# Cosine attention and a low-rank mixer: three query multiplies of the first batch on GpSimd, and the query and key copies of the same head pairs on VectorE alone

## The chip, the cores and the metric

The kernel runs on one core of one Trainium2 chip. The metric is the device time of one execution in microseconds (us). A time with "median" is the median of an experiment's timed runs; a profile shows one execution, and its span is some 2 us shorter than the time of the same run. The engines are called PE (TensorE), ACT (ScalarE), DVE (VectorE), POOL (GpSimd) and SP (SyncE); SBUF is the on-chip memory, PSUM the banks into which PE writes.

## The reference

```python
def _attn_ref(q, k, v, tau):                       # q, k, v: 8 x 12 x 448 x 64
    q_n = q / (np.linalg.norm(q, axis=-1, keepdims=True) + 1e-06)
    k_n = k / (np.linalg.norm(k, axis=-1, keepdims=True) + 1e-06)
    scores = np.matmul(q_n, k_n.transpose(0, 1, 3, 2)) / tau
    scores = scores - np.max(scores, axis=-1, keepdims=True)
    attn = np.exp(scores)
    attn = attn / (np.sum(attn, axis=-1, keepdims=True) + 1e-09)
    return np.matmul(attn, v)

def _moe_ref(x, U, V, w_ch1, w_ch2):               # x: 8 x 448 x 768, rank 32
    xt = x.transpose(0, 2, 1)
    h = xt @ U @ V
    u = x + h.transpose(0, 2, 1)
    ch = np.maximum(u @ w_ch1, 0.0) @ w_ch2        # 768 -> 3072 -> 768
    return u + ch
```

Twelve heads make six pairs (0 to 5) per batch. The change touches only batch 0, in the first 32 us of some 605.

## The kernel before

The kernel does not emit its instructions in the order of its source. It collects them as operations with an estimated duration and with dependences, and a small list scheduler simulates the five engines with these estimates when the kernel is built. The order it finds is then fixed for each engine. An operation marked "ACT/DVE" goes to whichever of the two the simulation finds free. So a change of one duration or one engine can rearrange everything behind it.

```python
def flip(stream, ins, n, into, part, deps, acq, rel, wide=1, eng="ACT/DVE", took=0.05):
    # PE transposes the blocks into PSUM, one copy brings them into qkT
    ...
    c = plan.add(Op(eng, any_t(n * len(ins) // wide, 2), None, deps=[o], acq=acq, rel=[tp],
                    prio=0.2, fast=True))
    c.fn = lambda: copy_op(c, *part(into(), tp.tile))
    return c
...
def scales(b, h0, h1, ld, ops, lo, ii, inv, pr, on, hold=()):
    # squares (ACT or DVE), sums (DVE), Ln and Exp (ACT), + EPS and reciprocal (DVE): inv, f32 in SBUF
    ...
def norm(b, p, ld, la, inv, a, deps, pr):          # one pair of heads
    ...
    def part(i, h0=0, h1=2):                       # i = 0: queries, i = 1: keys
        def fn():
            src = ...                              # 112 x 512, bf16, in SBUF
            sc = inv.tile[:, i, a + h0:a + h1, :].unsqueeze(3).to_broadcast([SCH, n, SC, D])
            ...
            nc.vector.tensor_mul(dst, src, sc)     # the unit queries or keys
        return plan.add(Op("DVE", dve_t(256 * (h1 - h0)), fn, deps=need + [deps[i]], acq=[xn],
                           rel=[ld, inv], prio=pr))
    ...
            done.append(flip(pe_tp, ..., [o], [qkT], [xn], 1, "ACT/DVE", 0.09 if first else 0.05))
```

The inverse norms are made for a third (four heads) at a time. Pairs 2 and 3 share a third, and so do pairs 4 and 5. Each pair then gives eight score matmuls and eight exponentials on ACT. GpSimd works through one list in the order of the source: it asks for all loads, and between them it clears tiles and casts the mixer's weights.

```python
    load_w1(0, 6)                                  # two of the four quarters of w1
    load_w1(6, 12)
    v_set = [plan.add(Op("POOL", 1.5, lambda t_=t_: set_v(t_)), pool_q) for t_ in v_t]
    consts = [ ...cast_u(0), cast_v, cast_u(1)... ]       # U and V to bf16
    state[0] = att(0)
    ...
    go(1, 0, 4)                                    # queries and keys of batch 1, heads 0 to 3
    load_w1(12, 18)                                # the third quarter
```

Of the kernel before, what the change touches and what calls it, by code (L numbers as in the profile page):

```python
# [204 lines left out]
def kernel(  # L205
# [12 lines left out]
    nc = tc.nc  # L218
# [95 lines left out]
    plan = Plan()  # L314
# [6 lines left out]
    pool_q = plan.stream("POOL")  # L321
# [7 lines left out]
    def dve_t(n, fast=1, fixed=0.065):  # L329
        return fixed + n * 0.00105 / fast  # L330
# [4 lines left out]
    def load(fn, busy, deps=(), acq=(), rel=(), late=2.0):  # L335
        return plan.add(Op("POOL", 0.71, fn, deps=deps, acq=acq, rel=rel,
                           lat=("in", busy, late)), pool_q)
# [7 lines left out]
    def load_w1(f0, f1):  # L345

        o = load(lambda: nc.gpsimd.dma_start(
            out=w1_sb[:, :, f0 * 128:f1 * 128],
            in_=moe_w_ch1.rearrange("(a p) f -> p a f", p=128)[:, :, f0 * 128:f1 * 128]),
            C * (f1 - f0) * 128 * 4 / 400e3)  # L350
        for f in range(f0, f1):
            w1_of[f] = o
# [8 lines left out]
    def flip(stream, ins, n, into, part, deps, acq, rel, wide=1, eng="ACT/DVE", took=0.05):  # L361


        tp = Slot(r_mm, 1)
        tp.own = True
        for z, x in enumerate(ins):
            def fn(z=z, x=x):
                if z == 0:
                    tp.tile = psum.tile([128, len(ins) // wide, n], BF, name="tp", tag="mm", bufs=3)
                m = 128 // wide  # L370
                nc.tensor.transpose(out=tp.tile[m * (z % wide):m * (z % wide + 1), z // wide, :], in_=x(),  # L371
                                    identity=ident[:n, :n])
            o = plan.add(Op("PE", took, fn, deps=deps + [id_set] if z == 0 else (), acq=[tp] + acq,
                            rel=rel if z == len(ins) - 1 else []), stream)
# [4 lines that stand above are left out]
# [5 lines left out]
    def load_qk(b, h0, h1, ld=None, lo=0, uses=None):  # L384

        ld = ld or Slot(r_ld, 4 if uses is None else uses)
        ops = [load(lambda i=i, src=src: nc.gpsimd.dma_start(  # L387
            out=ld.tile[:, i, lo:lo + h1 - h0, :],
            in_=src[b, h0:h1].rearrange("h (s c) d -> s h (c d)", c=SC)),
            (h1 - h0) * (0.31 if b else 0.35) + (1.2 if b == 0 and h0 == 4 and i == 0 else 0.0), acq=[ld], late=2.0 if b == 0 else LATE) for i, src in enumerate((q, k))]  # L390
        return ld, ops, lo
# [77 lines left out]
    def stats(b, h0, h1, ld, ops, lo, hold=()):  # L469

        pr = 0.3 + 0.03 * h0 if b == 0 else 4
        inv = Slot(r_inv, h1 - h0)
        o, _ = scales(b, h0, h1, ld, ops, lo, (0, 1), inv, pr, "DVE" if b else "ACT/DVE", hold)
        for p in range(h0 // 2, h1 // 2):
            o_ = norm(b, p, ld, lo + 2 * p - h0, inv, 2 * p - h0, {0: o, 1: o}, pr)
        return o_

    def stats_first(ld, ops):

        inv = Slot(r_inv, 3)  # L480
        done, ups = {}, []
        for i in range(2):
            done[i], up = scales(0, 0, 2, ld, ops, 0, (i,), inv, -1 - 0.1 * i, ("DVE", "ACT")[i])
            ups.append(up)
        return ups + norm(0, 0, ld, 0, inv, 0, done, -1)

    count = [0]

    def norm(b, p, ld, la, inv, a, deps, pr):


        by_pe = b < PE_BATCHES
        first = b == 0 and p == 0
        xn, qkT = Slot(r_xn, 3 if first else 2 if by_pe else 1), Slot(r_qkT, 8 if b == 0 else 7)
        need = [xn_set[count[0] % len(xn_t)]]
        count[0] += 1

        def part(i, h0=0, h1=2):
            def fn():
                n = h1 - h0  # L500
                src = ld.tile[:, i, la + h0:la + h1, :].rearrange("p h (c d) -> p h c d", d=D)
                sc = inv.tile[:, i, a + h0:a + h1, :].unsqueeze(3).to_broadcast([SCH, n, SC, D])
                if i == 0:
                    dst = xn.tile[:, 8:12, :].rearrange("p c (h d) -> p h c d", h=2)
                else:
                    dst = xn.tile.rearrange("p b e -> p (b e)")[:, 0:9 * 128].rearrange(
                        "p (h x) -> p h x", h=2)[:, h0:h1, 0:SC * 128].rearrange(
                        "p h (c e) -> p h c e", c=SC)[:, :, :, 0:D]
                nc.vector.tensor_mul(dst, src, sc)  # L509
            return plan.add(Op("DVE", dve_t(256 * (h1 - h0)), fn, deps=need + [deps[i]], acq=[xn],  # L510
                               rel=[ld, inv], prio=pr))

        if first:
            ops = [part(0), part(1, 0, 1), part(1, 1, 2)]
            blocks = [(8, 12, ops[0]), (0, 4, ops[1]), (4, 8, ops[2])]
        else:
            ops = [part(1), part(0)]
            blocks = [(0, 8, ops[0]), (8, 12, ops[1])]
        if not by_pe:
            done = [plan.add(Op("SP", 0.1, lambda: nc.sync.dma_start_transpose(  # L520
                out=qkT.tile, in_=xn.tile.rearrange("p b e -> p (b e)")), deps=ops, acq=[qkT],
                rel=[xn], prio=0, lat=("x", 0.05 * 84, LATE)))]
        else:
            done = []
            for b0, b1, o in blocks:
                done.append(flip(
                    pe_tp, [(lambda z=z: xn.tile[:, z, :]) for z in range(b0, b1)], SCH,
                    lambda: qkT.tile, (lambda t_, x, b0=b0, b1=b1: (t_[:, b0:b1, :], x)),
                    [o], [qkT], [xn], 1, "ACT/DVE", 0.09 if first else 0.05))
        got[b, p, "qkT"] = (qkT, lambda m: (done[0], done[1 + m // 4]) if first else done, done)  # L530
        return ops

# [273 lines left out]
    def set_v(t_):  # L806
        nc.gpsimd.memset(t_[:, :, 0:3, D:D + 2], 1.0)
        for hh in range(2):
            mine, other = slice(64 * hh, 64 * hh + 64), slice(64 - 64 * hh, 128 - 64 * hh)
            nc.gpsimd.memset(t_[mine, hh::2, 3, D:D + 2], 1.0)  # L810
            nc.gpsimd.memset(t_[other, hh::2, 3, :], 0.0)
# [22 lines left out]
    def cast_u(par):  # L834
        nc.gpsimd.tensor_copy(out=U_sb[:, par], in_=U_f()[:, par])
# [15 lines left out]
    def att(b):  # L851
        X = Slot(r_X, 0)
        muls = []
        for p in range(NPAIR):
# [4 lines left out]
    first = load_qk(0, 0, 2, uses=5)  # L859
    second = load_qk(0, 2, 4, first[0], 2)  # L860
    ld, ops, _ = load_qk(0, 4, 8)
# [6 lines left out]
                      deps=[zf, *begun], prio=-2, lat=12.0)) for t in range(4)]  # L868
# [3 lines left out]
    ld, ops, _ = load_qk(0, 8, 12)  # L872
# [2 lines left out]
    load_v0(8, 12)  # L875
    load_w1(0, 6)
    load_w1(6, 12)
    v_set = [plan.add(Op("POOL", 1.5, lambda t_=t_: set_v(t_)), pool_q) for t_ in v_t]
    consts = [plan.add(Op("POOL", 0.4, lambda: cast_u(0), deps=u0 + [z], rel=[uv]), pool_q),
              plan.add(Op("POOL", 1.2, cast_v, deps=v0 + [z], rel=[uv]), pool_q),  # L880
# [66 lines left out]
```

## Time and profile before

| what | value | how it is read |
|---|---|---|
| time, median of 4 runs beside the changed kernel | 608.19 us (607.26 to 608.47) | timed runs |
| profiled span | 605.0 us | that run took 607.15 us |
| reciprocal of the norms of heads 4 to 7 starts | 18.21 us | timeline, DVE |
| first MLP matmul starts | 39.40 us | timeline, PE |
| between these two, the **stretch** | 21.19 us | the part that the change touches |
| from the first MLP matmul to the end, the **rest** | 565.6 us | 605.0 - 39.4 |

I use the stretch and the rest throughout, because profiles start with different offsets: the reciprocal in question begins anywhere from 18.06 to 18.82 us in the thirteen profiles of the two kernels and the variants that the table below lists, whatever was changed. That offset of up to 0.76 us would drown the effect looked for; it drops out of the stretch.

### The profile page before, as it was taken

What the parts mean: (1) busy time and instruction counts of PE and PEld (TensorE: products, weight loads), DVE (VectorE), ACT (ScalarE), POOL (GpSimd) and SP (SyncE); (2) the same over time, 40 slices, a digit from 0 to 9 for tenths busy, and PEclk for the clock granted to TensorE, in tenths of its full rate; (3) what the DMA queues carried; (4) which work ended last, traced back from release to release, by engine and by line L of the source; (5) the groups of instructions that cost most, each with busy time, mean ns of one, the idle gap of its engine ahead of it and who ended that gap; (6) DMA issues with size and microseconds to landing.
All of it is one profiled execution on the core that took longest, in us unless ns stands there. A gap on an engine that the chain in (4) does not pass through costs nothing.

```text
span 605.0 us, 11545 instructions
## 1 busy us (share of the span) xinstructions
PE 587.7 (97%) x4731; PEld 348.6 (58%) x4731; DVE 295.6 (49%) x703; ACT 281.3 (46%) x606; POOL 120.9 (20%) x191
## 2 busy tenths in 40 slices
PE   4899999999999999999999999999999999999997
PEld 2565665555555665666445665666545666654565
DVE  8979669899998899644711253015300210110011
ACT  6977752488772286327641077506442015014300
POOL 8737234062611626000600000000000000000000
PEclk9999999999999999999999999999999999999999
DMA  9999997999998999724902141030002110310021
GB/s 121 191 206 113 205 197 96 151 150 145 123 113 151 183 153 143 98 67 84 157 0 66 43 89 41 1 93 27 15 1 53 52 40 1 88 43 1 0 53 53
DMA packets 150228, 54.58 MB, mean 90 GB/s; under 512 B 115104, under 2 KB 150176, under 8 KB 150176
## 3 DMA queue, kind: packets, MB, share of 16 engines
q0 software_dynamic: 73408, 25.96, 39.0%
q1 hardware_dynamic: 76704, 27.86, 24.7%
q8 instruction: 37, 0.61, 0.4%
q14 instruction: 15, 0.12, 0.1%
q10 hardware_dynamic: 64, 0.02, 0.0%
HBM read 52.25 MB, written 11.01 MB: 105 GB/s over the span
## 4 chain that ended last, share of the span: by engine, by line
PE 92%; ACT 5%; DVE 1%; DMA 0%; issue 0%; POOL 0%; ACTq 0%; POOLq 0%
PE mm L768 36%; PE mm L734 35%; PE sc L546 9%; PE av L566 7%; ACT attn L551 3%; PE mm L658 1%; ACT qkT L798 1%; PE mm L623 1%; PE tp L371 1%; ACT sq L438 1%; DVE xn L509 1%; PE sc L734 1%; DMA qk_nat<-in_k_dram 0%; ACT uT L798 0%; PE sc L658 0%
## 5 line engine op out<-in xcount | busy, mean ns | idle before, releaser
L734 PE MATMUL mm<-uT,w_sb 128*128 128x512 bf16 (+1 forms) x1134 | 236.5, 353 | 0.0
L768 PE MATMUL mm<-w_sb,relu 128*128 128x384 bf16 (+1 forms) x1368 | 233.4, 323 | 0.3 <-ACT uT L798 0.3
L551 ACT ACTIVATE attn<-sc 128x448 bf16<-128x448 f32 (+1 forms) x342 | 164.3, 565 | 98.0 <-PE av L566 66.4
L768 PEld LDWEIGHTS <-relu 128*128 128x128 bf16 x1368 | 132.6, 98 | 86.7 <-issue 0.9
L734 PEld LDWEIGHTS <-w_sb 128*128 128x128 bf16 x1152 | 112.2, 98 | 101.2 <-issue 0.8
L757 ACT ACTIVATE relu<-mm 128x384 bf16<-128x384 f32 (+1 forms) x172 | 93.9, 546 | 149.3 <-PE mm L734 148.9
L777 DVE TENSOR_TENSOR O_sb<-mm,u_nat 128x384 f32<-128x384 f32 (+1 forms) x57 | 31.1, 549 | 229.4 <-PE mm L768 222.6
L546 PE MATMUL sc<-qkT 128*128 128x448 bf16 (+1 forms) x342 | 105.8, 358 | 4.3 <-DVE qkT L800 1.3
L566 PEld LDWEIGHTS <-attn 128*128 128x128 bf16 (+1 forms) x1536 | 62.7, 98 | 17.7 <-issue 2.3
L409 POOL DMA_DIRECT2D v_nat<-in_v_dram x98 | 63.1, 650 | 35.4 <-DMA w_sb<-in_moe_w_ch_dram 9.7
L444 DVE TENSOR_REDUCE ss<-sq 112x8 f32<-112x512 bf16 x96 | 63.2, 673 | 1.1 <-ACT sq L438 0.7
L509 DVE TENSOR_TENSOR xn<-qk_nat,inv 112x512 bf16<-112x512 bf16 (+1 forms) x97 | 62.4, 676 | 0.3
L566 PE MATMUL av<-v_nat,attn 128*128 128x65 bf16 x1344 | 55.7, 193 | 0.0
L546 PEld LDWEIGHTS <-qkT 128*128 128x128 bf16 (+1 forms) x342 | 31.9, 103 | 24.1 <-issue 7.2
L387 POOL DMA_DIRECT2D qk_nat<-in_q_dram x25 | 17.8, 713 | 134.6 <-DVE xn L509 89.5
L575 DVE TENSOR_TENSOR X_sb<-av,rd 128x256 bf16<-128x256 f32 x96 | 40.2, 419 | 1.7
L573 DVE RECIPROCAL rd<-av 128x4 f32<-128x4 f32 x96 | 17.1, 179 | 38.2 <-PE av L566 37.4
L440 DVE TENSOR_TENSOR sq<-qk_nat 112x512 bf16<-112x512 bf16 x89 | 34.6, 413 | 0.9 <-DMA qk_nat<-in_q_dram 0.8
L672 DVE TENSOR_TENSOR u_nat<-mm,X_sb 128x384 bf16<-128x384 f32 x36 | 19.0, 552 | 11.1 <-PE mm L658 10.9
L371 PE MATMUL tp<-ident,xn 112*128 112x112 bf16 x144 | 11.1, 220 | 8.0 <-DVE xn L509 7.9
L387 POOL DMA_DIRECT2D qk_nat<-in_k_dram x25 | 17.6, 702 | 3.3 <-DMA w_sb<-in_moe_w_ch_dram 3.0
L457 ACT ACTIVATE ln<-ss 112x32 f32<-112x32 f32 (+2 forms) x26 | 6.1, 235 | 23.5 <-DVE ss L444 23.5
(60 smaller groups left out, 174.9 us busy)
## 6 DMA issues: line engine op xcount, KB each, us to landing
qk_nat<-in_q_dram POOLq DMA_DIRECT2D x23, 224.0 KB, 5.7
qk_nat<-in_k_dram POOLq DMA_DIRECT2D x23, 224.0 KB, 6.8
w_sb<-in_moe_w_ch_dram POOLq DMA_DIRECT2D x4, 1152.0 KB, 13.4
w_sb<-in_moe_w_ch_dram POOLq DMA_DIRECT2D x8, 576.0 KB, 16.2
out_dram<-O_sb SPq DMA_DIRECT2D x15, 168.0 KB, 2.2
out_dram<-O_sb SPq DMA_DIRECT2D x16, 144.0 KB, 2.1
out_dram<-O_sb SPq DMA_DIRECT2D x16, 120.0 KB, 2.0
out_dram<-O_sb SPq DMA_DIRECT2D x16, 96.0 KB, 2.2
```

What stands on the lines that cost most here:

```text
L387: ops = [load(lambda i=i, src=src: nc.gpsimd.dma_start(out=ld.tile[:, i, lo:lo + h1 - h0, :], in_=src[b, h0:h1].rearrange("h (s c) d -> s ...
L409: nc.gpsimd.dma_start(out=vb[p0:p0 + s1 - s0, hs, j, 0:D], in_=v[b, hs].rearrange("h (s c) d -> c s h d", c=SC)[c, s0:s1]),
L440: nc.vector.tensor_mul(y, x, x)
L444: lambda i=i, a0=a0, a1=a1, sq=sq: nc.vector.reduce_sum(ss.tile[:, i, a0:a1, :].rearrange("p h c -> p (h c)"), sq.tile[:, 0:a1 - a0, :].re ...
L509: nc.vector.tensor_mul(dst, src, sc)
L546: nc.tensor.matmul(out=sc.tile[0:rows_, 0:S], lhsT=kT[:, rows_ * m:rows_ * (m + 1)], rhs=qkT.tile[:, 8:12, :].rearrange("p c s -> p (c s)" ...
L551: exps[m] = plan.add(Op("ACT", act_t(S), lambda sc=sc, m=m: nc.scalar.activation(out=attn.tile[0:rows_, m, off:off + S], in_=sc.tile[0:row ...
L566: nc.tensor.matmul(out=av.tile[:, t, 0:D + 1], lhsT=attn.tile[0:rows_, m, 128 * t:128 * (t + 1)], rhs=vv[0:rows_, h, j, 0:D + 1], start=(j ...
L575: muls.append(plan.add(Op("DVE", dve_t(256), lambda av=av, rd=rd, h=h: nc.vector.tensor_mul(X.tile[:, :, h * D:(h + 1) * D], av.tile[:, :, ...
L734: o = plan.add(Op("PE", pe_t(n), lambda cc=cc: nc.tensor.matmul(out=mm.tile[:, 0:n], lhsT=w1_sb[:, cc, f * 128:(f + 1) * 128], rhs=uT.tile ...
L757: nc.scalar.activation(out=relu.tile[:, f, 0:n], in_=mm.tile[:, 0:n], func=AF.Relu)
L768: nc.tensor.matmul(out=mm.tile[:, 0:c1 - c0], lhsT=relu.tile[:, f, i * 128:(i + 1) * 128], rhs=w2.tile[:, f, c0:c1], start=(f == 0), stop= ...
```

## The change

The intent is to take work off ACT and DVE while batch 0 is bound by them. GpSimd makes the unit queries of pairs 3, 4 and 5, right after it has asked for the first half of w1. The copies of these pairs' transposed queries and keys out of PSUM are bound to DVE, so that ACT keeps to exponentials.

```diff
-    count = [0]
+    count, on_pool = [0], []
...
+        pooled = b == 0 and p >= 3
...
-                nc.vector.tensor_mul(dst, src, sc)
+                (nc.gpsimd if i == 0 and pooled else nc.vector).tensor_mul(dst, src, sc)
+            if i == 0 and pooled:
+                o = Op("POOL", 1.15, fn, deps=need + [deps[i]], acq=[xn], rel=[ld, inv])
+                on_pool.append(o)
+                return o
...
-                    [o], [qkT], [xn], 1, "ACT/DVE", 0.09 if first else 0.05))
+                    [o], [qkT], [xn], 1, "DVE" if b == 0 and p >= 3 else "ACT/DVE", 0.09 if first else 0.05))
...
     load_w1(6, 12)
+    for o in on_pool:
+        plan.add(o, pool_q)
     v_set = [...]
```

## The prediction

> **What bounds the kernel now.** I read the page first, then the chain of work that ended last, then busy time in stretches, then single instructions between 18 and 28 us. The page says that TensorE (PE) is the bound over the whole span, at full clock:
>
> ```profile
> PE 587.7 (97%) x4731; PEld 348.6 (58%) x4731; DVE 295.6 (49%) x703; ACT 281.3 (46%) x606; POOL 120.9 (20%) x191
> PE 92%; ACT 5%; DVE 1%; DMA 0%; issue 0%; POOL 0%; ACTq 0%; POOLq 0%
> ```
>
> The second line is the chain that ended last: ScalarE (ACT) holds only 5% of it, about 30 us. The change touches batch 0 alone, so the question is where those 30 us lie. Busy time by stretch answers it:
>
> ```profile
> 10.00:20.00 10.00, 7.98 (x68) 4.77 (x68) 9.59 (x24) 9.96 (x25) 8.95 (x19) 1.00 1.65 157
> 20.00:30.00 10.00, 9.12 (x141) 7.04 (x139) 9.09 (x25) 10.00 (x24) 6.21 (x11) 1.00 1.20 210
> 30.00:40.00 10.00, 9.80 (x130) 6.36 (x128) 6.01 (x17) 8.68 (x20) 3.73 (x6) 1.00 1.26 204
> 40.00:60.00 20.00, 18.88 (x141) 11.23 (x139) 18.71 (x40) 14.17 (x33) 12.61 (x19) 1.00 1.20 137
> ```
>
> After the window and its length the columns are PE, PEld, VectorE (DVE), ACT and GpSimd (POOL) busy us, then clock, DMA share and GB/s. From 10 to 30 us ACT is busy 19.96 of 20 and DVE 18.68 of 20: batch 0's attention is ACT-bound with DVE close behind. From about 40 us PE has MLP work to fill in and stays nearly full. So the end moves by what the start of that dense part (first MLP matmul, 39.4 us) moves, plus or minus what the rearranged order costs later.
>
> The chain of waits in the middle of batch 0:
>
> ```profile
> 20.66 0.80 ACT qkT L798
> 21.46 0.45 ACT attn L551
> 21.90 0.80 ACT qkT L798
> 22.82 0.43 ACT attn L551
> 23.38 2.60 ACT attn L551 x6
> 25.98 0.79 ACT qkT L798
> 26.77 5.65 ACT attn L551 x13
> ```
>
> Here L551 is the exponential and L798 the copy of transposed keys out of PSUM, 128x896. An exponential costs ACT 5.65/13 = 0.435 us in sequence, a key copy 0.80 (its own record says 0.96 to 1.05 because neighbours overlap). The copies at 21.90 and 25.98 belong to pairs 3 and 4. Pair 5's keys were already copied by DVE at 26.85, in 0.59 us.
>
> **What the Trainium skill says, and whether the trace agrees.** First, "GPSIMD Engine Reference", section 3.1, puts an elementwise instruction with two tensor inputs at about 2.6 cycles per element on GpSimd. At the page's 1.2 GHz my estimate for 512 elements is 512 x 2.6 / 1.2 = 1.11 us plus dispatch; DVE's multiply runs at 0.63 to 0.68 us in this trace. GpSimd has no such multiply in this kernel yet, so no run here shows it. The change's scheduler enters 1.15.
>
> Second, "SBUF — State Buffer", section "Who interferes with whom", says that a DVE instruction with two SBUF inputs contends with a GpSimd instruction that reads SBUF: one waits for the other. The multiplies of this change are exactly that pair. The trace of before agrees:
>
> ```profile
> 20.57 0.28 POOL L835 CAST U_sb<-raw_uv 128x128 bf16<-128x128 f32 x1
> 20.80 1.45 POOL L838 CAST V_sb<-raw_uv 128x448 bf16<-128x448 f32 x1
> 25.99 0.71 POOL L835 CAST U_sb<-raw_uv 128x128 bf16<-128x128 f32 x1 [3.74 <-DMA raw_uv<-in_moe_U_dram]
> 20.55 0.85 DVE L509 TENSOR_TENSOR xn<-qk_nat,inv 112x512 bf16<-112x512 bf16 x1
> ```
>
> The same U cast took 0.28 when it came first and 0.71 when it came inside a DVE multiply (24.05 to 26.55), and the DVE multiply that met the first cast took 0.85 instead of 0.68. Third, the same GPSIMD page's section 4.1 says GpSimd has no PSUM port, which is why POOL gets a multiply and not a copy.
>
> **The change, part by part.** (1) ACT loses two key copies. Of the six in batch 0 one was on DVE already; the instruction orders of the two kernels show 13 copies into qkT on ACT before and 11 after, 12 and 14 on DVE. By the chain that is 2 x 0.80 = 1.6 us. I give back 0.2: without the copy between them, the logarithm and the exponent of the last third's norms stand back to back and wait for each other. So 1.4 us at best, 39.4 to about 38.0.
>
> (2) DVE loses three multiplies (3 x 0.65 = 1.95 us) and gains two key copies (2 x 0.59 = 1.18). Net -0.8 us, on an engine that is 93% busy there.
>
> (3) POOL gains three multiplies, 3 x 1.15 = 3.45 us at the estimate, placed between the asking for w1 (ends 18.28) and the clearing of the v tiles. The first finds the inverse norms of heads 4 to 7 ready (18.55). The second and third must wait for those of heads 8 to 11, ready at 24.01 before, perhaps 23.4 after, since DVE has one multiply fewer ahead of them. So POOL is done at about 23.4 + 2.3 = 25.7 without contention. Then come the clears (18.25 to 20.57, so 2.3 us) and the casts (about 1.3): the next loads are asked for at about 29.5 to 31 instead of 26.65.
>
> (4) That delay should be hidden. The two w1 loads asked for at 16.6 keep the queue busy until about 32.5, when the second has landed:
>
> ```profile
> 32.48 0.53 POOL L409 DMA_DIRECT2D v_nat<-in_v_dram  x1 [0.58 <-DMA w_sb<-in_moe_w_ch_dram]
> ```
>
> The loads behind it slip by 0 to 1 us. Batch 1's queries landed at 33.6 and are first read at 39.7; the w1 quarter that landed at 40.4 is read at 59 (by counting matmuls, six to a slice). U and V casts move from 22.3 and 26.7 to about 30, first needed at 33.7. I charge nothing.
>
> (5) Contention. The order of after puts DVE's two key multiplies of pairs 4 and 5 right behind the inverse norms, and POOL starts its two query multiplies on the same signal: four instructions of 0.65, 0.65, 1.15 and 1.15 us. If the port is exclusive, they take 3.6 us one after the other instead of 2.3 side by side. PE runs its order rigidly: transposes of pair 4's keys, a score, pair 4's queries, pair 5's keys, two scores, pair 5's queries, scores. The eighth score of pair 2 is therefore behind all but one of the four multiplies: 23.4 + 3.0 for the multiplies + 0.5 for transposes, matmul and signals = 26.9. ACT wants it at 22.4 + 7 x 0.435 = 25.4. So up to 1.5 us of idle ACT. With little contention it is 0.2. At the first POOL multiply DVE's key multiply of pair 2 can be held up to 1.1 us, of which 0.5 to 0.7 reaches ACT. I charge 0.8 us for the two places, between the 0.2 and 2.2 that these add up to.
>
> Sum: -1.4 + 0.8 = -0.6 us, so 608.2 - 0.6 = 607.6.
>
> **Rivals.** *POOL's multiplies become the path* (exclusive port, POOL first each time): the charge is 2.2 or more, and the kernel ends at 609 to 610. For it speak the two slowed casts; against it, that they delayed by at most one multiply. *The ACT relief comes through whole* because the lock costs little: 606.8, and if the shorter order also trims PE's idle 1.12 us between 40 and 60 us, 605.9. For it: DVE's total falls and ACT had no idle time at all between 10 and 38 us. *Nothing comes through*, because PE itself is the limit from 32 us on: the chain there names PE scores and av matmuls in turn, with PE 9.80 of 10 busy between 30 and 40 us. Then relief on ACT is only waited out on PE: 608.2. *Loads arrive late*: the asking slips past the end of w1's transfer and the hole pushes w2. The w2 chunks landed up to 84.7 while the second MLP matmuls began at 82.3, but the last is needed only some 60 matmuls later, so I give this little weight.
>
> **Range and chances.** Best case -1.4 with up to 0.9 more from a luckier order; worst case +0.8 from the lock (2.2 - 1.4) and about 1 us of bad luck in the new order, since the scheduler rearranges everything behind. That gives 605.9 to 609.6. Two per cent is 12 us, far more than all terms together (the whole part touched lasts 30 us), so almost all the chance is on "within 2%".
>
> **What would show it.** POOL multiplies of 1.1 to 1.3 us where no DVE multiply runs, longer or with slowed DVE multiplies (above 0.8) where they meet: step 5. ACT's exponentials of pair 2 starting near 22.4 with a gap before the eighth: step 5's stall; without a gap: the rival of whole relief. First MLP matmul at 38.0 to 39.5 instead of 39.4: steps 1 and 5 together. POOL's first load behind the casts at 29.5 to 31 and the w1 quarter landing near 41: steps 3 and 4. The prediction is wrong if the difference at the first MLP matmul isn't that at the end (the order behind decided), or if PE waits for w1, w2 or batch 1's loads.

## The result and the profile after

The changed kernel takes 608.20 us (median of 4 runs, 608.01 to 608.71), the one before 608.19. The ratio is 1.0004, with a 95% interval from 0.9987 to 1.0021: the same. A ratio here is the mean time of one kernel's runs over the mean of the other's in the same rounds, so not quite the ratio of the medians. Later, five runs of the changed kernel against nine of the kernel before gave 1.0013 (1.0001 to 1.0026).

The page of the changed kernel, busy time by engine and the chain that ended last by engine:

```profile
PE 588.8 (97%) x4731; PEld 348.8 (57%) x4731; DVE 295.7 (49%) x703; ACT 281.1 (46%) x603; POOL 124.2 (20%) x194
PE 91%; ACT 4%; DVE 3%; DMA 1%; issue 1%; POOL 0%; ACTq 0%; POOLq 0%
```

POOL has three instructions and 3.3 us more. DVE has as many instructions as before and is as busy as before (295.7 against 295.6), although it gave three multiplies away and got only two of the shorter key copies for them (the third instruction is a copy of u that is split in two). That is the first sign: its own multiplies got longer. In the chain, ACT fell from 5% to 4% and DVE rose from 1% to 3%.

Busy time by stretch of the changed kernel and then, in the last line, of the kernel before; columns as in the prediction:

```profile
20.00:30.00 10.00, 8.83 (x129) 6.42 (x129) 9.63 (x24) 8.70 (x20) 5.45 (x14) 1.00 1.21 211
...
30.00:32.00 2.00, 1.91 (x26) 1.25 (x25) 1.17 (x4) 2.00 (x6) 2.00 (x5) 1.00 0.28 49
...
30.00:32.00 2.00, 1.90 (x24) 1.07 (x22) 0.76 (x3) 2.00 (x6) 1.90 (x3) 1.00 1.31 194
```

Between 20 and 30 us ACT is now busy for 8.70 of 10 us; before it was 10.00. DVE is busy for 9.63 instead of 9.09. ACT was relieved, and part of the relief stands there as idle time. The DMA engines carry 49 GB/s between 30 and 32 us; the kernel before has 194 there. That is a hole in the loads.

ACT's timeline of the changed kernel; the columns are start, duration, engine, line, operation with its tiles, number of instructions, and in brackets the idle time before with what ended it:

```profile
22.73 0.23 ACT L457 ACTIVATE ln<-ss 112x32 f32<-112x32 f32 x1
23.00 0.23 ACT L460 ACTIVATE ln<-ln 112x32 f32<-112x32 f32 x1
23.37 3.25 ACT L556 ACTIVATE attn<-sc 112x448 bf16<-112x448 f32 x7
27.53 11.48 ACT L556 ACTIVATE attn<-sc 112x448 bf16<-112x448 f32 x25 [0.91 <-PE sc L551]
```

After seven exponentials ACT waits 0.91 us for the eighth score of pair 2. What PE itself waited for is seen in the chain of waits of the changed kernel (start, length, what):

```profile
24.55 2.14 DVE xn L510 x2
26.74 0.57 PE tp L371 x8
27.30 0.20 PE sc L551
27.53 5.85 ACT attn L556 x13
```

Two DVE multiplies take 2.14 us, then eight transposes and one score follow, and only then can ACT go on. Here are the multiplies that met, as POOL's and then DVE's timeline of the changed kernel have them:

```profile
19.25 1.04 POOL L510 TENSOR_TENSOR xn<-qk_nat,inv 112x512 bf16<-112x512 bf16 x1 [1.18 <-DVE inv L465]
24.65 2.93 POOL L510 TENSOR_TENSOR xn<-qk_nat,inv 112x512 bf16<-112x512 bf16 x2 [4.37 <-PE av L571]
...
31.21 0.78 POOL L387 DMA_DIRECT2D qk_nat<-in_q_dram  x1
43.78 0.69 POOL L409 DMA_DIRECT2D v_nat<-in_v_dram  x1 [5.42 <-DMA w_sb<-in_moe_w_ch_dram]
...
19.35 2.68 DVE L510 TENSOR_TENSOR xn<-qk_nat,inv 112x512 bf16<-112x512 bf16 x3
24.54 2.14 DVE L510 TENSOR_TENSOR xn<-qk_nat,inv 112x512 bf16<-112x512 bf16 x2
```

In the kernel before, the same timelines of DVE, ACT and POOL show:

```profile
18.75 2.65 DVE L509 TENSOR_TENSOR xn<-qk_nat,inv 112x512 bf16<-112x512 bf16 x4
...
24.05 2.50 DVE L509 TENSOR_TENSOR xn<-qk_nat,inv 112x512 bf16<-112x512 bf16 x4
...
26.50 11.54 ACT L551 ACTIVATE attn<-sc 112x448 bf16<-112x448 f32 x25
...
40.42 0.69 POOL L409 DMA_DIRECT2D v_nat<-in_v_dram  x1 [4.51 <-DMA w_sb<-in_moe_w_ch_dram]
```

Four multiplies took DVE 2.65 us before, and the next four 2.50; now three take 2.68 and two 2.14. One of them met POOL's first. At 24.54 two meet POOL's second and third, and all four get slow: 1.07 each on DVE, 1.47 each on POOL.

The sums of the two profiles: the stretch goes from 21.19 to 40.36 - 18.82 = 21.54 us, so +0.35 instead of the predicted -0.6. The rest goes from 565.6 to 606.9 - 40.36 = 566.5, so +0.9. The +0.35 taken alone is less than the stretch varies from profile to profile (21.19 and 21.91 us for the same instructions, see before_late); the waits inside it, and the kernels below, have to say what happened.

### The profile page after: what moved, and what is told of

Same layout as the page of the kernel before. It is cut to its first block, busy times and chain, and to the rows that moved or that the text cites. A ratio compares the mean times of both kernels' runs of the same rounds, so it can differ in the third digit from the quotient of the medians.

```text
span 606.9 us, 11544 instructions
## 1 busy us (share of the span) xinstructions
PE 588.8 (97%) x4731; PEld 348.8 (57%) x4731; DVE 295.7 (49%) x703; ACT 281.1 (46%) x603; POOL 124.2 (20%) x194
## 4 chain that ended last, share of the span: by engine, by line
PE 91%; ACT 4%; DVE 3%; DMA 1%; issue 1%; POOL 0%; ACTq 0%; POOLq 0%
PE mm L773 36%; PE mm L739 34%; PE sc L551 9%; PE av L571 7%; ACT attn L556 3%; DVE xn L510 1%; PE mm L663 1%; PE mm L628 1%; DMA qk_nat<-in_k_dram 1%; DVE ss L444 1%; PE sc L739 1%; ACT qkT L803 0%; PE tp L371 0%; ACT sq L438 0%; DVE qkT L805 0%
## 5 line engine op out<-in xcount | busy, mean ns | idle before, releaser
L762 ACT ACTIVATE relu<-mm 128x512 bf16<-128x512 f32 (+1 forms) x172 | 94.1, 547 | 149.0 <-PE mm L739 148.3
```

What stands on the lines that cost most here:

```text
L762: nc.scalar.activation(out=relu.tile[:, f, 0:n], in_=mm.tile[:, 0:n], func=AF.Relu)
```

## The experiments

The leading theory (A) is that the two engines' multiplies collide when both of their inputs lie in SBUF, and that this costs the stretch what ACT gains. Its rivals are that something else limits the stretch, DVE's own load or PE, so that relief on ACT cannot come through at all (B); and that the loads asked for later leave a hole which is paid for behind (C), possibly together with the rearranged order. Twelve runs were made: ten new kernels, and two repeats; none failed but micro, whose result is wrong.

| kernel | stretch | rest | median us (runs) | ratio to before, 95% interval |
|---|---|---|---|---|
| before | 21.19 | 565.6 | 608.19 (4) | |
| after | 21.54 | 566.5 | 608.20 (4) | 1.0004, 0.9987 to 1.0021 |
| after_again (the same kernel) | 21.55 | 566.5 | 608.33 (5) | 1.0013, 1.0001 to 1.0026 |
| copies_only | 21.26 | 565.8 | 607.31 (6) | 0.9996, 0.9979 to 1.0014 |
| pool_only | 21.69 | 566.4 | 608.25 (6) | 1.0009, 0.9997 to 1.0022 |
| asks_first | 22.99 | 566.3 | 609.56 (6) | 1.0022, 1.0006 to 1.0037 |
| asks_between | 22.70 | 566.1 | 608.92 (6) | 1.0022, 1.0010 to 1.0034 |
| psum_inv | 19.94 | 567.05 | 607.04 (5) | 0.9989, 0.9978 to 1.0001 |
| psum_between | 20.12 | 565.5 | 606.35 (5) | 0.9979, 0.9967 to 0.9991 |
| best_again (psum_between again) | 19.94 | 565.4 | 605.53 (5) | 0.9971, 0.9958 to 0.9985 |
| psum_between_free | 20.55 | 566.05 | 606.93 (5) | 0.9987, 0.9974 to 0.9999 |
| before_late | 21.91 | 565.6 | 607.71 (5) | 0.9999, 0.9985 to 1.0012 |
| engines_only | 22.41 | 565.5 | 608.07 (5) | 1.0009, 0.9996 to 1.0021 |

The kernel before had medians of 607.92, 607.69, 607.68 and 607.47 us. A profile is one run and repeats well in the rest (after 566.5 twice, psum_between 565.5 and 565.4), less well in the stretch. So where a profile and the timed ratio disagree by some tenths, the ratio is the average over the runs.

### copies_only: no multiply on POOL

```diff
-        pooled = b == 0 and p >= 3
+        pooled = False
```

> The copies of pairs 3 to 5 by VectorE alone, the three query multiplies back on VectorE. Measured from the start of the reciprocal that makes the inverse norms of heads 4 to 7 to the first MLP matmul, the kernel before takes 21.19 us and the changed one 21.54. Theory A (the multiplies on GpSimd collide with VectorE's key multiplies at a shared port and eat what the copies gave ScalarE): without collisions the stretch is 20.3 to 20.8 us, no gap of 0.9 us before the eighth exponential of pair 2, time 0.999 of before or less. Theory B (taking copies from ScalarE gives nothing, since VectorE or TensorE is as full): 21.1 to 21.6 us, ratio 1.000 to 1.002. Theory C (the late asking for loads is what costs): the asking is back at about 27 us here, the queue has no hole at 30 to 34 us, and the ratio is below that of the changed kernel by 0.001 or more even if the stretch is unchanged.

The copies of pairs 3 to 5 are on DVE, all multiplies too. DVE's and then ACT's timeline of copies_only:

```profile
19.35 3.44 DVE L510 TENSOR_TENSOR xn<-qk_nat,inv 112x512 bf16<-112x512 bf16 x4
...
23.72 0.23 ACT L457 ACTIVATE ln<-ss 112x32 f32<-112x32 f32 x1 [1.22 <-DVE ss L444]
```

The first four multiplies took 3.44 us instead of 2.65: two of them met POOL's casts of U (at 20.56 us) and V (20.80, 1.45 long), where in the profile of before only one did. DVE came late to the sum of squares of the next third, and ACT waited 1.22 us for it. The stretch is 21.26, as before, and the ratio 0.9996: the copies alone gain nothing measurable. That is the number that the rival B expects for this kernel, and not the 20.3 to 20.8 of A. But this profile has a collision with the casts of its own, so it does not show that DVE's load is the reason, nor whether B explains the changed kernel.

### pool_only: the multiplies on POOL, the copies free again

```diff
-    [o], [qkT], [xn], 1, "DVE" if b == 0 and p >= 3 else "ACT/DVE", 0.09 if first else 0.05))
+    [o], [qkT], [xn], 1, "ACT/DVE", 0.09 if first else 0.05))
```

> The three query multiplies on GpSimd, the copies free for ScalarE or VectorE as before. Theory A: the collisions stay and the relief of ScalarE is gone, the stretch is 22 to 23 us and the time 1.001 to 1.004 of before. Theory B: VectorE has less to do, and the stretch is 20.5 to 21.2, ratio 0.998 to 1.000. Theory C: like the changed kernel in time (hole in the queue at 30 to 34 us), 1.000 to 1.001.

The stretch is 21.69, the rest 566.4. So the multiplies on POOL bring the collisions (DVE's two take 2.14 us, POOL's two 2.93) and the longer rest without the copies. The stretch lies between what A (22 to 23) and B (20.5 to 21.2) expected, so it decides between neither. The rest already points to the order or the hole, since copies_only has neither the hole (198 GB/s between 30 and 34 us, against 91 in pool_only) nor much of the loss (565.8).

### asks_first and asks_between: the next loads before the multiplies

Both ask for batch 1's first queries and keys and for the third quarter of w1 early. asks_first does so ahead of all three POOL multiplies, asks_between after the first one (`on_pool[0]` before these lines, `on_pool[1:]` after them).

```diff
     load_w1(6, 12)
+    early = load_qk(1, 0, 4)
+    load_w1(12, 18)
     for o in on_pool:
         plan.add(o, pool_q)
...
-    go(1, 0, 4)
-    load_w1(12, 18)
+    stats(1, 0, 4, *early, hold=after)
```

> The changed kernel with batch 1's first queries and keys and the third quarter of w1 asked for ahead of GpSimd's multiplies, which closes the hole in the load queue and starts the first multiply about 1 us later. Theory A: the time hardly moves (0.999 to 1.001 of before); VectorE's multiplies still take about 1.5 us where they meet GpSimd's. Theory C: the DMA share at 30 to 34 us is back above 1.1, and what the changed kernel lost behind the first MLP matmul (about 0.9 us against before in the two profiles) comes back: ratio 0.998 to 0.999.

> The changed kernel with the asking for batch 1's first queries and keys and w1's third quarter between GpSimd's first and second multiply, where GpSimd waits 4.4 us for the norms of heads 8 to 11. Theory A: collisions and the gap of about 0.9 us stay, stretch 21.4 to 21.7. Theory C (the hole in the load queue costs time behind the first MLP matmul): the DMA share from 30 to 34 us is above 1.1 (0.44 in the changed kernel) and the ratio is 0.9985 to 0.9995. If the hole costs nothing, the ratio stays at 1.000 to 1.001, as that of the changed kernel.

The hole closed in both: the DMA share between 30 and 34 us is 1.33. Yet both are slower than before (1.0022). In asks_first, POOL's first multiply came while two DVE multiplies ran and took 1.49 instead of 1.04 us, and ACT had gaps of 0.58, 0.31, 0.78 and 0.90 us. In asks_between the gaps were 0.59, 1.10 and 0.86. Their profiles also caught something else, here in the busy time by stretch of asks_between:

```profile
21.00:22.00 1.00, 1.00 (x13) 0.77 (x12) 0.98 (x3) 0.90 (x2) 0.79 (x1) 0.50 1.17 200
22.00:23.00 1.00, 1.00 (x18) 1.00 (x16) 0.39 (x2) 0.80 (x4) 0.00 (x0) 0.50 1.28 212
```

The granted clock is 0.50 in these rows. The half clock lasted 3.41 us in each of the two profiles. The Trainium skill, "TensorE: Matmul & The Clock Gate", section "What's actually happening", names two clock states, full and half, and a window of about 3.4 us over which PE's activity is judged. The profile agrees with both. That it was the waits of PE just before that brought the drop is only argued. So these two stretches are not to be compared with the others. The drop is not the whole loss: by the mean clock of a run it can be present in three of six runs of asks_first (0.997) and two of six of asks_between (0.996 and 0.997), while the others, at 0.999 or 1.000, still took 607.79 to 609.53 and 607.94 to 609.36 us. What follows is that closing the hole alone is no gain while the multiplies collide.

### micro: the collision by itself (wrong results on purpose)

> Not the computation, a wrong result on purpose: the same multiply (112x512 bf16 by broadcast float32) measured by itself: four on GpSimd alone; eight on VectorE alone; both at once; VectorE with its second input in PSUM alone and at once with GpSimd; VectorE reducing with one input at once with GpSimd. Theory A (a port shared by GpSimd's reads and VectorE's second SBUF input): GpSimd 1.04 us alone and about 1.5 when both run, VectorE 0.65 alone and about 1.5 for each that meets a GpSimd one; with the second input in PSUM, and for the reductions, both as alone. A rival that any simultaneous work slows both: slowed in the PSUM and reduce phases too.

This kernel computes nothing useful; it was run once. It has 112x512 multiplies with a broadcast second operand, as in the kernel: four on POOL alone, eight on DVE alone, both together; then DVE with its second operand in PSUM, alone and together with POOL; then, after one more multiply of two SBUF operands, DVE sums beside POOL.

```python
def mul(eng, dst, src, inv):
    eng.tensor_mul(dst.rearrange("p (c d) -> p c d", d=D), src.rearrange("p (c d) -> p c d", d=D),
                   inv.unsqueeze(2).to_broadcast([P, N // D, D]))
```

Its timeline, the rows of the five multiply phases:

```profile
2.54 4.04 POOL L28 TENSOR_TENSOR p_pool<-src_p,inv_pool 112x512 bf16<-112x512 bf16 x4 [2.10 <-ACT inv_pool L37]
...
7.07 4.91 DVE L28 TENSOR_TENSOR d_dve<-src_d,inv_dve 112x512 bf16<-112x512 bf16 x8 [5.14 <-ACT inv_dve L37]
...
12.30 8.29 DVE L28 TENSOR_TENSOR d_both<-src_d,inv_both 112x512 bf16<-112x512 bf16 x8 [0.32 <-ACT inv_both L37]
12.34 5.89 POOL L28 TENSOR_TENSOR p_both<-src_p,inv_both 112x512 bf16<-112x512 bf16 x4 [5.76 <-ACT inv_both L37]
...
25.29 4.86 DVE L28 TENSOR_TENSOR d_both<-src_d,ips_both 112x512 bf16<-112x512 bf16 x8
...
25.74 4.04 POOL L28 TENSOR_TENSOR p_both<-src_p,inv_both 112x512 bf16<-112x512 bf16 x4 [7.50 <-ACT inv_both L37]
```

Alone, a POOL multiply costs 4.04 / 4 = 1.01 us and a DVE multiply 4.91 / 8 = 0.61. Together, POOL needs 5.89 / 4 = 1.47 each, and DVE's eight take 3.38 us longer, 0.85 for each of the four meetings. With DVE's second operand in PSUM there is no change at all: 4.86 and 4.04, as alone (DVE alone with PSUM took 4.86 too). DVE's eight sums of 112x512 elements, which have one tensor input, took 4.84 beside POOL. POOL's four multiplies of that phase took 4.55 us, 0.51 more than alone, about what one meeting costs (0.46), and one multiply of DVE opens the phase. So the sums leave POOL alone; the sums by themselves were not run. This is the rule that the SBUF page of the prediction gives, with prices: while four POOL multiplies meet four of DVE, a pair takes 1.47 us, against 1.01 + 0.61 = 1.62 strictly one after the other and 1.01 fully side by side.

### psum_inv: the same kernel without collisions

The remedy from micro, put into the changed kernel. For heads 4 to 11 a second reciprocal writes the inverse norms into a slot of a PSUM ring. DVE's multiplies read them there, POOL's read the copy in SBUF. Nothing is taken away that makes a wait; the data lie elsewhere. The scheduler, told of two more reciprocals, also moved some transposes and attention matmuls in PE's order, so it is not the changed kernel to the last instruction.

```diff
+            o1 = plan.add(Op("DVE", 0.2, lambda: nc.vector.reciprocal(
+                inv.tile[:, 0:1, 0:g, :], nv.tile[:, 0:1, 0:g, :]), deps=[o], acq=[inv], rel=[nv], prio=pr))
+            o2 = plan.add(Op("DVE", 0.3, lambda: nc.vector.reciprocal(
+                ips_of(ips)[:, 0:2, 0:g, :], nv.tile[:, 0:2, 0:g, :]), deps=[o], acq=[ips], rel=[nv], prio=pr))
...
+            by = inv if ips is None or (i == 0 and pooled) else ips
-                sc = inv.tile[:, i, a + h0:a + h1, :].unsqueeze(3).to_broadcast([SCH, n, SC, D])
+                sc = (by.tile if by is inv else ips_of(ips))[:, i, a + h0:a + h1, :].unsqueeze(3).to_broadcast([SCH, n, SC, D])
```

> The changed kernel, but VectorE's multiplies of pairs 2 to 5 take the inverse norms from a PSUM tile, so that they have one SBUF input and don't meet GpSimd's multiplies at the shared port; that costs two more reciprocals of about 0.2 us. GpSimd takes them from SBUF as before. VectorE's order is otherwise that of the changed kernel. Theory A (collisions eat the gain): GpSimd's three multiplies take 1.0 to 1.1 us each, VectorE's first three 1.9 to 2.0 together (2.68 in the changed kernel) and its next two 1.3 (2.14); the gap of 0.91 us before the eighth exponential of pair 2 falls to 0.3 or less; the stretch from the reciprocal of heads 4 to 7 to the first MLP matmul is 20.3 to 20.9 us (21.54 in the changed kernel, 21.19 before), ratio 0.998 to 1.000. Rival (TensorE is the limit from 32 us on): collisions and gap vanish, but the stretch stays at 21.1 to 21.6.

The timelines of DVE, POOL and ACT in psum_inv:

```profile
18.80 1.87 DVE L529 TENSOR_TENSOR xn<-qk_nat,mm 112x512 bf16<-112x512 bf16 x3
...
23.29 1.28 DVE L529 TENSOR_TENSOR xn<-qk_nat,mm 112x512 bf16<-112x512 bf16 x2
...
23.18 2.05 POOL L529 TENSOR_TENSOR xn<-qk_nat,inv 112x512 bf16<-112x512 bf16 x2 [3.71 <-DVE inv L470]
...
22.09 14.61 ACT L575 ACTIVATE attn<-sc 112x448 bf16<-112x448 f32 x32
```

Three DVE multiplies take 1.87 us instead of 2.68, two 1.28 instead of 2.14, POOL's two 2.05 instead of 2.93. ACT runs 32 exponentials without a gap where the changed kernel had 7, a wait of 0.91 and 25. The stretch is 19.94 us: 1.6 below the changed kernel, and 1.25 below the kernel before, although DVE has two reciprocals more (20.3 to 20.9 was expected). This refutes the rival that PE is the limit from 32 us on, and it refutes B for the changed kernel: relief of this size does come through to the first MLP matmul when the multiplies do not collide. But the rest is 567.05, longer by 0.5 than that of the changed kernel, so the timed gain is only 0.1% and its interval reaches 1.0001.

### psum_between and psum_between_free: with the loads early, and with the copies free

psum_between is psum_inv with the early loads of asks_between. psum_between_free is the same with the copies back to "ACT/DVE".

> Both of the above at once. Theory A alone: as the kernel with the inverse norms in PSUM, ratio 0.998 to 1.000. Theories A and C: the stretch is 20.3 to 20.9 and the hole closed, ratio 0.997 to 0.999. Rival (neither matters, TensorE is the limit): 1.000 to 1.001.

> The fastest so far (inverse norms in PSUM for VectorE, asking between GpSimd's multiplies), but with the copies of pairs 3 to 5 free for ScalarE or VectorE as before the change. If the relief of ScalarE is what paid (two copies of 0.80 us), the stretch grows from 20.12 to 20.9 to 21.7 us and the ratio to before is 0.999 to 1.000. If relieving VectorE by GpSimd's multiplies paid instead, the stretch stays at 20.0 to 20.4 and the ratio at 0.9975 to 0.9985.

psum_between: stretch 20.12, rest 565.5, ratio 0.9979. It is faster than the kernel before, with an interval that excludes 1, though well within 2%. In psum_between_free one key copy is on ACT again (25.25 us, 0.96 long), the stretch is 20.55 and the ratio 0.9987. So the second half of the change, the copies on DVE alone, is worth about 0.4 to 0.6 us in the stretch, but only where DVE is free of collisions; in copies_only it was worth nothing. The 20.55 us lie between the two expectations (20.9 to 21.7 if ACT's relief paid, 20.0 to 20.4 if DVE's did), and the other copy stayed on DVE, so what is left, 21.19 - 20.55 = 0.64 us, is not split between that copy and the multiplies on POOL. One control is missing: the kernel before with its inverse norms in PSUM. It would lose its own collisions with POOL's casts too. In the profile of before these cost little (2.65 + 2.50 us for eight multiplies, against 8 x 0.62 = 5.0 us at the pace of psum_inv), but before_late, next, shows a worse case; so part of the timed gain of psum_between need not be the change's.

### before_late: the kernel before, with its loads asked for later

Ten clears of an unused tile in POOL's list hold back the loads. The scheduler is told that they take 0.001 us, and the orders of PE, ACT, DVE and SP stay what they were.

```diff
+    for _ in range(10):
+        plan.add(Op("POOL", 0.001, lambda: nc.gpsimd.memset(idle_t, 0.0)), pool_q)
     state[0] = att(0)
```

> The kernel before with ten idle clears (about 4 us) on GpSimd between the U and V casts and the asking for batch 1's loads, and no other change: the hole alone. Theory C (the hole in the load queue costs time behind the first MLP matmul): the stretch stays at 21.1 to 21.3 us, the DMA share from 30 to 34 us falls below 0.9, and the ratio is 1.0008 to 1.0025. If the hole costs nothing: 0.9995 to 1.0005.

Busy time of before_late between 30 and 34 us, and its first multiplies on DVE:

```profile
30.00:34.00 4.00, 3.81 (x57) 2.49 (x54) 1.64 (x5) 4.00 (x11) 3.73 (x6) 1.00 0.70 83
```

```profile
18.63 3.61 DVE L510 TENSOR_TENSOR xn<-qk_nat,inv 112x512 bf16<-112x512 bf16 x4
```

The hole is there (83 GB/s; the changed kernel has 55), the loads are asked for at 30.27 us, and GpSimd asks for the load that waits for the third quarter of w1 at 43.41, that is 25.3 us behind the reciprocal, against 25.0 in the changed kernel and 22.2 before. Still the rest is 565.6, as before, and the ratio 0.9999. So the hole by itself costs nothing: C falls, as far as it is the hole alone. The second fence is a by-catch. Ahead of the ten clears the program is the same, and yet the four multiplies that took 2.65 us in the profile of before take 3.61 here: POOL's casts of U and V began 1.8 us behind the reciprocal and not 2.4, and one multiply had to wait out both. The kernel before has its own collisions, in some runs more than in others. This adds about 0.7 us to this stretch (21.91 against 21.19).

### engines_only: the changed engines in the order of before

The scheduler plans the kernel before; only when the instructions are emitted do the three multiplies go to GpSimd and the copies of pairs 3 to 5 to DVE. PE's and SP's orders are those of before.

```diff
-                nc.vector.tensor_mul(dst, src, sc)
+                (nc.gpsimd if i == 0 and b == 0 and p >= 3 else nc.vector).tensor_mul(dst, src, sc)
...
+        def fn():
+            if dve:
+                nc.vector.tensor_copy(*part(into(), tp.tile))
+            else:
+                copy_op(c, *part(into(), tp.tile))
```

> The change with the order of the kernel before: the scheduler plans as before, and only when the instructions are written do the three query multiplies go to GpSimd (now between the clears and the U and V casts) and pair 3's and 4's key copies to VectorE. TensorE's order is that of before to the last instruction. Theory D (the changed kernel loses about 0.9 us behind the first MLP matmul because its order there is another): from the first MLP matmul to the end 565.4 to 565.9 us, as before (565.6), against 566.5 in both profiles of the changed kernel. Rival (the loss comes with the GpSimd multiplies or the late asking, whatever the order): 566.2 or more. The stretch before it: GpSimd's multiplies still collide, 21.0 to 22.2 us.

ACT's timeline of engines_only:

```profile
23.12 0.55 ACT L556 ACTIVATE attn<-sc 112x448 bf16<-112x448 f32 x1 [0.46 <-PE sc L551]
...
29.52 10.09 ACT L556 ACTIVATE attn<-sc 112x448 bf16<-112x448 f32 x22 [1.27 <-PE sc L551]
```

In this order POOL's third multiply comes behind the V cast, only at 27.67, and ACT waits 1.27 us for what hangs on it; the stretch is 22.41, a little above the 21.0 to 22.2 expected. The rest is 565.5, as in the kernel before. So the 0.9 us of the changed kernel behind its first MLP matmul come with the rearranged order, not with the engines on which the work runs. (This kernel has no hole, 191 GB/s between 30 and 34 us; before_late has the hole in the same order, and asks_first and asks_between have none in another one, with rests of 566.3 and 566.1.)

### after_again and best_again

The changed kernel and psum_between, run again beside engines_only.

> The changed kernel again, on the same chip as the two others and with more rounds. Ratio 1.000 to 1.0015, stretch 21.4 to 21.7; the gap of about 0.9 us before the eighth exponential of pair 2 and GpSimd's two multiplies of 1.48 us again.

> The fastest kernel again: inverse norms in PSUM for VectorE, asking between GpSimd's multiplies. Ratio 0.997 to 0.999, stretch 20.0 to 20.3 us, from the first MLP matmul to the end 565.3 to 565.8.

Both repeat. The changed kernel has a stretch of 21.55 and a rest of 566.5 (21.54 and 566.5 the first time), psum_between 19.94 and 565.4 (20.12 and 565.5). psum_between's ratio is 0.9971 (0.9958 to 0.9985), 605.53 us: the fastest kernel.

## Why the prediction was right or wrong

The class was right, and the measured 608.20 lies in the range from 605.9 to 609.6. The predicted point, 607.6, was too low by 0.6 us: a gain was predicted, and none was measured. (The upper end does not follow from its own terms: 608.2 + 0.8 + 1 = 610.0, not 609.6. Nothing hangs on it.) By its steps:

**Step 1, ACT's relief of 1.4 us: right.** Without collisions the stretch falls from 21.19 to 19.94 us (psum_inv and again best_again), so by 1.25, and the two extra reciprocals of DVE are in that. In the profiles of before and of psum_inv the timeline lists no gap of ACT from the reciprocal to the last exponential (38.04 and 36.70 us), and the first MLP matmul starts 1.36 and 1.35 us behind it. So the 1.25 us went out of ACT's own list, as the prediction has it. One copy given back to ACT (psum_between_free) costs 0.4 to 0.6 us, less than the 0.80 that the prediction counts for each.

**Step 2, DVE's net -0.8 us: right by count, not in effect.** The three multiplies left, but those that stayed grew by nearly as much, and DVE's busy time is unchanged to 0.1 us.

**Step 3, POOL: right.** A multiply took 1.04 us on its own against the 1.15 of the estimate. The next loads were asked for at 31.21, or 30.6 once the offset of 0.6 us between the profiles is taken off: inside the 29.5 to 31 predicted, although POOL's two colliding multiplies were each 0.46 longer than alone.

**Step 4, loads later but without a charge: the size was off, the charge was right.** I predicted a slip of 0 to 1 us. The load that waits for the third quarter of w1 was asked for at 43.78 instead of 40.42, which is 2.7 us later once the same offset is taken off. My reason was that the queue stays busy with the two quarters already asked for until 32.5. They were hardly done sooner (the second took 14.41 us from asking to landing, 14.75 before). But before, the next loads were asked for at 26.65, 5.5 us ahead of that landing at 32.19; in the changed kernel at 31.21, 0.4 us ahead of the landing at 31.62, and by then the queue had run empty: by single microseconds the changed kernel moves 207 to 216 GB/s from 26 to 30 us, 95 in the next and 3 in the one after, where the kernel before goes on at 193 and 195. What the new loads carried came to 30 and 92 GB/s from 32 to 34 us. before_late shows that this costs nothing: the same kind of hole, rest 565.6, ratio 0.9999.

**Step 5, the collisions: this term of the sum was mis-sized.** The mechanism and its place were right: a wait before the eighth exponential of pair 2, 0.91 us long, and a smaller loss at POOL's first multiply. I charged 0.8 us for both. The difference between the changed kernel and psum_inv, in which the collisions are gone, is 21.54 - 19.94 = 1.6 us: 0.9 at the second place, 0.6 at the first (ACT starts its seven exponentials at 23.37 - 18.82 = 4.55 us after the reciprocal, in psum_inv at 22.09 - 18.11 = 3.98), and the remaining 0.1 is not pinned to one wait. It lies within the 0.2 to 2.2 that I named, but I took a middle value because I did not know how exclusive the conflict is. micro shows that it is nearly so: 1.47 us for a pair against 1.62 in series. With 1.6 in the place of 0.8, the sum is -1.4 + 1.6 = +0.2; the profiles say +0.35.

**The order behind: I put this into the range, not into the sum.** "About 1 us of bad luck" was allowed for, and 0.9 came, shown as the order's by engines_only against after_again (rest 565.5 against 566.5). This is also the condition under which I had called the prediction wrong in its reasoning: the difference at the first MLP matmul is not the one at the end. The two profiles together give +0.35 + 0.9 = 1.25 us. The timed ratios give less, 0.04% and 0.13%, which is 0.2 to 0.8 us, and one reason can be seen: the profiled run of before, 607.15 us, is a good one (median 608.19), while its own collisions with POOL's casts cost it 0.7 us in a run such as before_late. That the timed runs of before vary for this reason is argued; only single profiles were kept.

**The rivals.** "POOL's multiplies become the path" did not happen: the kernel is at 608.2 and not at 609 to 610, and the charge was 1.6, not 2.2. "The relief comes through whole" is what psum_inv's stretch does, once the collisions are gone. "PE is the limit from 32 us on" is refuted by the same stretch. "Loads arrive late" is refuted by before_late.

**What stays open.** Why the new order costs 0.9 us in the rest, and 1.5 us in psum_inv, is not pinned to an instruction. Up to the last matmul it is 562.1 us from the first MLP matmul before and 563.0 in after_again, with the same 4392 matmul records in both. The place can be narrowed down by comparing the two traces at points where both have run the same matmuls: after_again is level with before 24.1 us behind the first MLP matmul, 0.41 us later at 43.7, 0.64 at 62.0, 0.98 at 107.6, and still 0.98 at the end (the profile of after gives the same to 0.01). So the loss arises between 24 and 108 us, well after the hole has closed, and the order behind costs nothing. PE's idle time in the first 440 us differs by only 0.2 (2.3 against 2.5 us). Most of the extra time is recorded as PE being busy with the same matmuls in another order. Since psum_between has a rest of 565.5 with an order of its own, such an amount is within what the scheduler deals out by chance; that it is chance is argued, not shown.

## What to carry to other kernels

Before moving a multiply to GpSimd to relieve VectorE, look at what VectorE does at that moment: if both read two tensors from SBUF, they run nearly one after the other (1.47 us for a pair here), and instructions released by the same signal meet (here they started 0.11 us apart). If VectorE's small second operand can be put into PSUM, the conflict disappears (here at the price of two more reciprocals of 0.24 to 0.30 us), and only then do the other parts of such a change, here the copies bound to VectorE, show what they are worth. And in a kernel ordered by a scheduler, compare the stretch that was changed and everything behind it separately, since a reshuffled order can give or take as much as the change itself.

## What the Trainium skill lacked or had wrong

- "SBUF — State Buffer", section "Who interferes with whom", describes this conflict as an exclusive lock and gives no price for this pair of instructions. The runs agree with the rule and show a little less than full exclusion: a pair takes 1.47 us against 1.62 in series; a meeting costs a 0.61 us VectorE multiply 0.85 us more and a 1.01 us GpSimd multiply 0.46 more. The page has the case of one SBUF input, but not the remedy that follows from it: with the second operand in PSUM both ran as if alone (4.86 and 4.04 us).
- The same section says that the issue order decides who waits. When both come close together, the recorded starts do not tell it: in before_late a VectorE multiply recorded from 19.83 us took 1.81 us, while the casts recorded from 19.87 and 20.11 took 0.28 and 0.98. The page does not say what this does to a kernel's spread: four VectorE multiplies in the same order took 2.65 us in one profile and 3.61 in another.
- "GPSIMD Engine Reference", section 3.1, measures about 2.6 cycles per element for two inputs, 1.11 us for 512 elements by my estimate. With a second operand that is broadcast along 64 elements, the runs show 1.01 to 1.04 us. The page does not have this case.
